# Opening of a fused attention and mixer kernel: who loads the constants, who casts first, and when a channel weight's transfer is issued

## The chip, the cores and the metric

The kernel runs on one core of a Trainium2 chip. The metric is the device time of one execution in microseconds (us); less is better. The core has five engines that run their own instruction streams and meet through semaphores: TensorE (PE; its weight loads are listed as PEld), VectorE (DVE), ScalarE (ACT), GpSimd (POOL) and SyncE (SP). Transfers between the chip's memory and the core are issued from the streams of SP, ACT and POOL, and all of them are carried by the same 16 DMA engines.

## The reference

A batch of 8 goes through windowed attention and then through a mixer. Four heads see the last 32 positions, four see every fourth of the last 128.

```python
# B, H, S, D = 8, 8, 576, 64
scores = (q @ k.T) / sqrt(D)
mask_plain = (rel >= 0) & (rel < 32)                      # heads 0 to 3
mask_dil = (rel >= 0) & (rel < 128) & (rel % 4 == 0)      # heads 4 to 7
attn = softmax(where(mask, scores, -1e9))
x = (attn @ v) as [B, S, 512]
h = relu(x.T @ w_tok1) @ w_tok2        # mixing over the 576 positions, inner width 256
u = x + h.T
out = u + relu(u @ w_ch1) @ w_ch2      # mixing over the 512 channels, inner width 1536
```

Inputs and output are float32; the kernel computes in float16 with float32 sums.

## The kernel before

One program handles the eight batches one after the other. For each batch it transposes q and k on TensorE (later batches by DMA), forms the scores in blocks near the diagonal, takes the exponential on ScalarE, multiplies with v (`av`), normalises on VectorE (`xn`), mixes over positions (`h1p`, `up`), turns the result (`tpu`) and mixes over channels: `gp` is the product with `w_ch1` (tiles `w3[0]` to `w3[2]`, four of twelve blocks `mb` each; in the trace they are all called `w`), `yp` the one with `w_ch2`. The order is written by hand: the stream of every engine is the order of the calls, and no engine goes past an instruction that waits. From batch 0's `gp` on, the attention of batch b+1 is interleaved into the main stream of batch b, by due times that are fixed in the code; the first transposes of batch 1 (`tp_q`, `tp_k`) stand between the first blocks of batch 0's `gp`.

Everything ahead of that is the opening, lines 840 to 1001, on which the change works. Its parts:

- Loads of q and k of batch 0 are issued in turn by SP and ACT (lines 843 to 850), in pieces of two, two and four heads, with the last 64 positions ("tails", tile `lt`) between them; then SP issues v (`load_v`, lines 199 to 220): four pieces `l_vn` for heads 0 to 3, the tail `l_vt`, two pieces `l_vd` for heads 4 to 7, and `l_vx`, their positions 384 to 511. A transfer issued by SP or ACT takes one of eight completion semaphores in turn; the ninth waits until the first has landed.
- The constants (identity, permutation, masks) come by POOL's queue (line 840).
- POOL casts most of what lands from float32 to float16 (lines 866 to 882), and between these casts it issues the weights' transfers, which convert on the way: `w1p`, `w1t`, `w2`, and with `load_w3` the channel weights `w3[0]` (line 878, ahead of the casts of `l_vd`) and `w3[1]` (line 881, between the casts of `l_vd` and `l_vx`).
- Line 884 copies `w2` into `w2p`. Line 974 is a gate: a copy of one element of `w2p[1]` into batch 1's tile `lt`, so that SP's loads of batch 1 (lines 975 to 980) are issued only after the second of these copies. Batch 1's casts on POOL start at line 981, with the third channel weight (line 984) between the first casts.
- `emit_fixed` and `emit_fixed_late` write the zeros and ones that stay: `qz` and `kt` on VectorE, the whole of `attt` on VectorE, the ones columns of both batches' `vv` and `vt` and the zeros of `w1t` on POOL.
- `warm` (line 831) issues matmuls on zeros, nine before the first transpose.

Of the kernel before, what the change touches and what calls it, by code (L numbers as in the profile page):

```python
# [16 lines left out]
S = 576  # L17
# [51 lines left out]
def kernel(  # L69
# [11 lines left out]
    nc = tc.nc  # L81
# [4 lines left out]
    def fixed(name, shape, dtype=FP16):  # L86
        return sb.tile(shape, dtype, tag=name, bufs=1, name=name)
# [28 lines left out]
    const = fixed("const", [128, CW])  # L116
# [12 lines left out]
    const_dram = nc.inline_tensor(const_np, name="consts").ap()  # L129
# [8 lines left out]
    vv = [fixed(f"vv{i}", [128, 5, H, 65]) for i in range(2)]  # L138
    vt = [fixed(f"vt{i}", [128, 4, 65]) for i in range(2)]
# [3 lines left out]
    attt = fixed("attt", [128, 4, 2, TW])  # L143
# [3 lines left out]
    w1t = [fixed(f"w1t{i}", [128, DTOK]) for i in range(2)]  # L147
    w2a = fixed("w2", [128, 2, 640])
# [10 lines left out]
    def emit_fixed():  # L159
        nc.gpsimd.memset(idle, 0.0)  # L160
        nc.gpsimd.memset(spread, 0.0)
        nc.vector.memset(qza[64:128, :, 0], 0.0)
        nc.vector.memset(qza[0:64, :, 1], 0.0)
        nc.vector.memset(kta[:, :, S:640], 0.0)
        for a in attp:
            nc.gpsimd.memset(
                a.rearrange("p h (b c) -> p h b c", c=PST)[:, :, :, 128:PST], 0.0)
        nc.vector.memset(attt, 1.0)

    def emit_fixed_late():  # L170
        for i in range(2):
            nc.gpsimd.memset(vv[i][64:128, 4], 0.0)
            nc.gpsimd.memset(vv[i][:, :, :, 64:65], 1.0)
            nc.gpsimd.memset(vt[i][:, :, 64:65], 1.0)
            nc.gpsimd.memset(w1t[i], 0.0)
        nc.gpsimd.memset(w2a[:, :, S:640], 0.0)


    l32 = {}
# [8 lines left out]
    def load_qk(b, nm, h0, h1, eng):  # L188
        i = h0 // 4
        eng.dma_start(  # L190
            out=l32[(b, nm, i)][:, h0 - 4 * i:h1 - 4 * i].rearrange("m h r d -> m h (r d)"),
            in_=SRC[nm][b, h0:h1, 0:512, :].rearrange("h (m r) d -> m h (r d)", r=4))

    def load_tail(b, nm, eng):
        r0 = 64 * (nm == "k")
        eng.dma_start(out=l32[(b, "t")][r0:r0 + 64],
                      in_=SRC[nm][b, :, 512:S, :].rearrange("h s d -> s h d"))
# [53 lines left out]
    def cast_qk(b, nm, hp, eng):  # L251
        if (b, nm) not in c16:
            c16[(b, nm)] = sb.tile([128, 4, 4, 2, D], FP16, tag=f"c_{nm}", bufs=1, name=f"c_{nm}_{b}")
        copy(eng, c16[(b, nm)][:, hp],
             l32[(b, nm, hp // 2)][:, 2 * (hp % 2):2 * (hp % 2) + 2].rearrange("m h r d -> m r h d"))
# [151 lines left out]
    def first_tails():  # L407

        p = bank("fl", 3, "tp_t", FP16)
        for hp in range(4):  # L410
            nc.tensor.transpose(
                out=p[:, 128 * hp:128 * hp + 128],
                in_=c16[(0, "t")][:, 2 * hp:2 * hp + 2, :].rearrange("m h d -> m (h d)"), identity=ident)
        t = p[:, 0:512].rearrange("p (x n c) -> p x n c", n=2, c=64)
        for h in range(2):
            rows = slice(64 * h, 64 * h + 64)
            nc.vector.tensor_copy(out=qza[rows, :, h, 512:S], in_=t[rows, :, 0])
        nc.vector.tensor_copy(out=kta[:, :, 512:S], in_=t[:, :, 1])
# [412 lines left out]
    def warm(n):  # L831

        p = bank("main", 3, "idle_p")
        for _ in range(n):
            nc.tensor.matmul(out=p, lhsT=idle[:, 0:128], rhs=idle, start=True, stop=True)
# [1 line left out]
    ctx.enter_context(tc.manual_schedule())  # L837


    nc.gpsimd.dma_start(out=const, in_=const_dram)  # L840
    emit_fixed()
    new_qk(0)
    load_qk(0, "q", 0, 2, nc.sync)
    load_qk(0, "k", 0, 2, nc.scalar)
    load_qk(0, "q", 2, 4, nc.sync)
    load_qk(0, "k", 2, 4, nc.scalar)
    load_tail(0, "q", nc.sync)
    load_tail(0, "k", nc.scalar)
    load_qk(0, "q", 4, 8, nc.sync)
    load_qk(0, "k", 4, 8, nc.scalar)  # L850
    spark = fixed("spark", [1, 1], FP32)
    nc.scalar.activation(out=spark, in_=idle[0:1, 0:1], func=AF.Exp)
    load_v(0)
# [1 line left out]
    def gate(t, src):  # L855
        nc.gpsimd.tensor_copy(out=t, in_=src)

    def load_w3(i):
        c = slice(512 * i, 512 * i + 512)
        nc.gpsimd.dma_start(out=w3[i], in_=moe_w_ch1[:, c].rearrange("(x p) c -> p x c", p=128))  # L860

    cast_qk(0, "q", 0, nc.scalar)
    cast_qk(0, "k", 0, nc.vector)
    nc.vector.tensor_scalar(out=veil, in0=const[:, 256:CW], scalar1=1.0, scalar2=60000.0,
                            op0=ALU.subtract, op1=ALU.mult)
    cast_qk(0, "q", 1, nc.gpsimd)
    emit_fixed_late()
    cast_tails_qk(0, nc.gpsimd)
    nc.gpsimd.dma_start(out=w1p, in_=moe_w_tok1[0:512, :].rearrange("(m r) j -> m r j", r=4))
    for hp in range(2, 4):  # L870
        cast_qk(0, "q", hp, nc.gpsimd)
    nc.gpsimd.dma_start(out=w1t[0][0:64], in_=moe_w_tok1[512:S, :])
    nc.gpsimd.tensor_copy(out=spread[:, 3:515:4], in_=ident)
    cast_qk(0, "k", 3, nc.gpsimd)
    for s in range(4):
        cast_vn(0, s, nc.gpsimd)
    nc.gpsimd.dma_start(out=w2a[:, :, 0:S], in_=moe_w_tok2.rearrange("(p j) t -> p j t", j=2))
    load_w3(0)
    cast_vd(0, 0, nc.gpsimd)
    cast_vd(0, 2, nc.gpsimd)  # L880
    load_w3(1)
    cast_vx(0, nc.gpsimd)
    nc.gpsimd.dma_start(out=w1t[1][64:128], in_=moe_w_tok1[512:S, :])
    for jb in range(2):
        nc.gpsimd.tensor_copy(
            out=w2p[jb], in_=w2[jb][:, 0:512].rearrange("p (m r) -> p r m", r=4))

    warm(9)
    ts = [st[2] for st in score_steps(0, 0.0, 1.0)]
    va = [st[2] for st in value_steps(0, 0.0, 1.0)]  # L890

    def tp(hp):
        ts[5 * hp]()
        ts[5 * hp + 1]()

    def sc(hp):
        for i in range(2, 5):
            ts[5 * hp + i]()

    def natural_w1(i):  # L900
        p = bank("main", 3, f"w1_p{i}")
        for s in (2 * i, 2 * i + 1):
            for r in range(4):
                nc.tensor.matmul(out=p[:, 256 * (s % 2):256 * (s % 2) + 256],
                                 lhsT=spread[:, 128 * s + 3 - r:128 * s + 131 - r], rhs=w1p[:, r],
                                 start=(r == 0), stop=(r == 3))
        copy(nc.scalar, w1n[:, 2 * i:2 * i + 2].rearrange("p s j -> p (s j)"), p)
# [3 lines left out]
    ts[2]()  # L911
    ts[3]()
    cast_qk(0, "k", 1, nc.vector)
    tp(1)
    first_tails()
    ts[7]()
    ts[8]()
# [8 lines left out]
    va[0]()  # L926
    va[1]()
    sc(3)
    va[2]()
    va[3]()  # L930
    natural_w1(0)
    natural_w1(1)
    for h in range(4, 8):
        va[h]()
# [37 lines left out]

    new_qk(1)
    gate(l32[(1, "t")][0:1, 0, 0:1], w2p[1][0:1, 0, 0:1])
    for nm in ("q", "k"):
        load_tail(1, nm, nc.sync)
    for h0 in (0, 4):
# [9 lines left out]
    for i in range(3):  # L987
        nc.gpsimd.dma_start(
            out=w4a[:, 4 * i:4 * i + 4],
            in_=moe_w_ch2[512 * i:512 * i + 512, :].rearrange("(p i) c -> p i c", i=4))  # L990
# [82 lines left out]
```

## Time and profile before

| what | us |
|---|---|
| median of 3 runs (range) | 288.43 (288.23 to 289.59) |
| the profiled execution, its own time | 289.66 |
| span of the trace, first to last instruction | 287.8 |
| PE busy in the span | 276.8 (96%) |
| POOL, ACT, DVE busy | 163.0, 134.0, 132.1 |

The page of the profile has a row of busy tenths in 40 slices of 7.2 us each. PE has 5, 8 and 7 tenths in the first three slices and 9 from then on but for the last. So what the opening costs stands in the first 22 us. The DMA row of the same page has 9 in nearly every slice of the first half, so transfers there stand in line for the DMA engines, and which transfer is issued first matters.

In the views, `x4` is the number of merged instructions, the time in a timeline row is when the first starts and for how long they go on, and what stands in brackets is how long the engine had been idle before and what ended that. For transfers the last number is the time from issue to landing.

### The profile page before, as it was taken

What the parts mean: (1) busy time and instruction counts of PE and PEld (TensorE: products, weight loads), DVE (VectorE), ACT (ScalarE), POOL (GpSimd) and SP (SyncE); (2) the same over time, 40 slices, a digit from 0 to 9 for tenths busy, and PEclk for the clock granted to TensorE, in tenths of its full rate; (3) what the DMA queues carried; (4) which work ended last, traced back from release to release, by engine and by line L of the source; (5) the groups of instructions that cost most, each with busy time, mean ns of one, the idle gap of its engine ahead of it and who ended that gap; (6) DMA issues with size and microseconds to landing.
All of it is one profiled execution on the core that took longest, in us unless ns stands there. A gap on an engine that the chain in (4) does not pass through costs nothing.

```text
span 287.8 us, 6995 instructions
## 1 busy us (share of the span) xinstructions
PE 276.8 (96%) x2838; PEld 210.9 (73%) x2838; DVE 132.1 (46%) x278; ACT 134.0 (47%) x265; POOL 163.0 (57%) x221
## 2 busy tenths in 40 slices
PE   5879999999999999999999999999999999999995
PEld 2777676888766886698776976797766966886594
DVE  7747658446764236414640164416440274421022
ACT  2854673263543804574447615482546534225500
POOL 6961860478865799449970999279952930000000
PEclk9999999999999999999999999999999999999999
DMA  7999999993999998979888978299974210431023
GB/s 218 263 211 218 283 225 207 320 218 82 328 210 192 264 264 230 139 164 350 226 159 182 330 224 186 57 219 329 193 150 95 85 64 2 91 112 37 0 76 108
DMA packets 105551, 52.63 MB, mean 183 GB/s; under 512 B 73872, under 2 KB 104464, under 8 KB 105520
## 3 DMA queue, kind: packets, MB, share of 16 engines
q1 hardware_dynamic: 101280, 47.07, 67.0%
q0 software_dynamic: 2640, 3.94, 8.0%
q10 hardware_dynamic: 1600, 1.18, 1.4%
q8 instruction: 22, 0.36, 0.6%
q14 instruction: 9, 0.07, 0.1%
HBM read 37.07 MB, written 9.44 MB: 162 GB/s over the span
## 4 chain that ended last, share of the span: by engine, by line
PE 80%; DMA 8%; DVE 3%; POOL 3%; issue 2%; ACT 2%; ACTq 1%; SPq 0%; POOLq 0%; DVEq 0%
PE yp L787 29%; PE gp L768 24%; DMA l_vd<-in_v_dram 4%; PE h1p L627 4%; PE yp L807 3%; DMA l_k<-in_k_dram 3%; PE up L639 3%; PE sc L510 3%; PE gt L759 3%; DVE xn L112 1%; DMA kr<-c_k 1%; PE h1p L625 1%; PE av L608 1%; PE up L650 1%; PE av L603 1%
## 5 line engine op out<-in xcount | busy, mean ns | idle before, releaser
L787 PE MATMUL yp<-w,gt 128*128 128x256 f16 x756 | 87.1, 273 | 0.0
L787 PEld LDWEIGHTS <-gt 128*128 128x128 f16 x768 | 78.6, 106 | 6.5
L106 ACT ACTIVATE gt<-gp 128x512 f16<-128x512 f32 x69 | 41.2, 597 | 76.3 <-PE gp L768 76.0
L768 PE MATMUL gp<-utd,w 128*128 128x512 f16 x144 | 54.7, 380 | 0.0
L768 PE MATMUL gp<-utm,w 128*128 128x512 f16 x144 | 54.6, 379 | 0.0
L768 PEld LDWEIGHTS <-w 128*128 128x128 f16 x384 | 39.2, 114 | 20.3 <-issue 0.5
L797 DVE TENSOR_TENSOR o<-yp,u 128x512 f32<-128x512 f32 x31 | 21.4, 691 | 63.1 <-PE yp L787 58.5
L112 POOL TENSOR_TENSOR attp<-attp,const 128x1280 f16<-128x1280 f16 x12 | 31.4, 2616 | 27.5 <-ACT attp L534 27.4
L112 DVE TENSOR_TENSOR xn<-av,rec 128x320 f16<-128x320 f32 x64 | 31.4, 491 | 2.2
L112 POOL TENSOR_TENSOR attd<-attd,const 128x1024 f16<-128x1024 f16 x12 | 25.3, 2132 | 1.6 <-ACT attd L534 1.6
L768 PE MATMUL gp<-uT,w 128*128 128x512 f16 x96 | 25.8, 379 | 0.0
L108 DVE TENSOR_SCALAR gt<-gp 128x512 f16<-128x512 f32 x27 | 18.5, 686 | 13.6 <-PE gp L768 13.1
L645 DVE TENSOR_TENSOR u<-up,xn 128x512 f16<-128x512 f32 x26 | 17.9, 690 | 7.5 <-PE up L639 7.5
L534 ACT ACTIVATE attp<-sc 128x480 f16<-128x480 f32 (+1 forms) x36 | 16.1, 536 | 7.4 <-PE sc L510 7.4
L102 POOL CAST c_k<-l_k 128x512 f16<-128x512 f32 x29 | 18.0, 628 | 1.9 <-DMA l_k<-in_k_dram 1.7
L102 POOL CAST c_q<-l_q 128x512 f16<-128x512 f32 x27 | 16.8, 629 | 3.1 <-DMA l_q<-in_q_dram 3.1
L616 DVE RECIPROCAL rec<-av 128x5 f32<-128x5 f32 x64 | 12.2, 190 | 13.8 <-PE av L613 13.7
L106 ACT ACTIVATE h<-h1p 128x256 f16<-128x256 f32 x29 | 11.1, 384 | 14.5 <-PE h1p L627 14.1
L399 POOL COPY kt<-kr 128x512 f16<-128x512 f16 x10 | 10.7, 1075 | 9.0 <-DMA kr<-c_k 9.0
L697 ACT COPY utd<-utm 128x512 f16<-128x512 f16 x12 | 12.8, 1135 | 4.1 <-DMA utm<-u 4.1
L102 POOL CAST vv<-l_vn 128x256 f16<-128x256 f32 x32 | 12.0, 420 | 4.3 <-DMA l_vn<-in_v_dram 4.1
L112 POOL TENSOR_TENSOR attt<-attt,const 128x512 f16<-128x512 f16 x12 | 14.0, 1165 | 0.0
(147 smaller groups left out, 459.9 us busy)
## 6 DMA issues: line engine op xcount, KB each, us to landing
out_dram<-o SPq DMA_DIRECT2D x72, 128.0 KB, 3.1
l_q<-in_q_dram SPq DMA_DIRECT2D x15, 512.0 KB, 7.2
l_k<-in_k_dram SPq DMA_DIRECT2D x14, 512.0 KB, 7.1
l_vn<-in_v_dram SPq DMA_DIRECT2D x32, 128.0 KB, 6.6
l_vd<-in_v_dram SPq DMA_DIRECT2D x16, 256.0 KB, 4.6
w<-in_moe_w_ch_dram POOLq DMA_DIRECT2D x6, 512.0 KB, 7.6
lt<-in_q_dram SPq DMA_DIRECT2D x8, 128.0 KB, 4.6
l_vt<-in_v_dram SPq DMA_DIRECT2D x8, 128.0 KB, 4.9
```

Of the source, the lines that this page charges most:

```text
L102: eng.tensor_copy(out=out, in_=in_)
L106: nc.scalar.activation(out=out, in_=in_, func=AF.Relu)
L108: eng.tensor_scalar_max(out=out, in0=in_, scalar1=0.0)
L112: eng.tensor_tensor(out=out, in0=x, in1=y, op=ALU.mult)
L534: nc.scalar.activation(out=out, in_=in_, func=AF.Exp, scale=0.125)
L616: nc.vector.reciprocal(out=rec[:, :, 0], in_=av[:, :, 64])
L627: nc.tensor.matmul(out=p, lhsT=w[:, s, j], rhs=x[:, s, c], start=False, stop=(s == 3))
L645: nc.vector.tensor_tensor(out=u16(b, s), in0=blocks4(p), in1=blocks4(xn[b][:, s]), op=ALU.add)
L697: nc.scalar.copy(out=natural(uTd[:, cb - 2]), in_=uTm[i][:, cb].rearrange("p r m -> p m r"))
L768: nc.tensor.matmul(out=p, lhsT=w3_block(cb, mb), rhs=uT[(b, cb)][0], start=(i == 0), stop=(i == 3))
L787: nc.tensor.matmul(out=p[:, c], lhsT=gta[:, mb, a0:m0 + 512:4] if half else gta[:, mb, a0:a0 + 128], rhs=w4[mb][:, c], start=(mb == 0), st ...
L797: nc.vector.tensor_tensor(out=blocks4(o32), in0=blocks4(p), in1=u16(b, s), op=ALU.add)
```

## The change

The constants are issued by SP as its second transfer instead of by POOL as its first. VectorE takes the first cast of q from ScalarE. The whole-tile write of `attt` becomes two calls of `emit_ones`, three small writes each, put behind the second cast of k and behind the second pair of transposes. The fixed writes for batch 1's buffers (`emit_fixed_late(1)`) and the second load of `w1t` go behind the gate. On POOL, the cast of k's last pair goes ahead of the copy into `spread`, the cast of `l_vx` goes ahead of both channel weights, and `load_w3(0)` goes behind the three casts of v, next to `load_w3(1)`. The first row of warm matmuls has seven instead of nine, and the first `natural_w1` stands ahead of the third `values` step.

```diff
-        nc.vector.memset(attt, 1.0)
+    def emit_ones(hp):
+        t = attt[:, 2 * hp:2 * hp + 2].rearrange("p a h c -> p (a h) c")
+        nc.vector.memset(t[:, :, 0:64], 1.0)
+        nc.vector.memset(t[:, :, 128:192], 1.0)
+        nc.vector.memset(t[:, :, 256:320], 1.0)
...
-    nc.gpsimd.dma_start(out=const, in_=const_dram)
     emit_fixed()
     new_qk(0)
     load_qk(0, "q", 0, 2, nc.sync)
     load_qk(0, "k", 0, 2, nc.scalar)
+    nc.sync.dma_start(out=const, in_=const_dram)
...
-    cast_qk(0, "q", 0, nc.scalar)
+    cast_qk(0, "q", 0, nc.vector)
...
-    emit_fixed_late()
+    emit_fixed_late(0)
...
     nc.gpsimd.dma_start(out=w2a[:, :, 0:S], in_=moe_w_tok2.rearrange("(p j) t -> p j t", j=2))
-    load_w3(0)
     cast_vd(0, 0, nc.gpsimd)
     cast_vd(0, 2, nc.gpsimd)
+    cast_vx(0, nc.gpsimd)
+    load_w3(0)
     load_w3(1)
-    cast_vx(0, nc.gpsimd)
-    nc.gpsimd.dma_start(out=w1t[1][64:128], in_=moe_w_tok1[512:S, :])
...
-    warm(9)
+    warm(7)
...
     cast_qk(0, "k", 1, nc.vector)
+    emit_ones(0)
     tp(1)
+    emit_ones(1)
...
     sc(3)
+    natural_w1(0)
     va[2]()
     va[3]()
-    natural_w1(0)
...
     gate(l32[(1, "t")][0:1, 0, 0:1], w2p[1][0:1, 0, 0:1])
+    emit_fixed_late(1)
+    nc.gpsimd.dma_start(out=w1t[1][64:128], in_=moe_w_tok1[512:S, :])
```

First place: POOL, from the load of `w2` (tile `w_81`) to batch 1's first cast. `w_0_84` and `w_1_85` are the first two channel weights, `lt_589` and `lt_587` the gate's target. Before:

```order
L877 DMA w_81<-in_moe_w_tok_dram 128x2x576
L860 DMA w_0_84<-in_moe_w_ch_dram 128x4x512
L102 CAST vv_69<-l_vd_123 128x4x2x64 [waits DMAHW5_49]
L102 CAST vv_69<-l_vd_123 128x4x2x64 [waits DMAHW6_49]
L860 DMA w_1_85<-in_moe_w_ch_dram 128x4x512
L102 CAST vt_71<-l_vx_124 128x4x64 [waits DMAHW7_49]
L883 DMA w1t_80<-in_moe_w_tok_dram 64x256 [waits Pool_49]
L885 COPY w2p_82<-w_81 128x512 [waits DMASW3_49]
L885 COPY w2p_83<-w_81 128x512
L856 CAST lt_589<-w2p_83 1x1 [waits Pool_49]
```

Now the same stretch reads:

```order
L882 DMA w_81<-in_moe_w_tok_dram 128x2x576
L102 CAST vv_69<-l_vd_122 128x4x2x64 [waits DMAHW6_49]
L102 CAST vv_69<-l_vd_122 128x4x2x64 [waits DMAHW7_49]
L102 CAST vt_71<-l_vx_123 128x4x64 [waits DMAHW0_49]
L865 DMA w_0_84<-in_moe_w_ch_dram 128x4x512
L865 DMA w_1_85<-in_moe_w_ch_dram 128x4x512
L889 COPY w2p_82<-w_81 128x512 [waits DMASW2_49]
L889 COPY w2p_83<-w_81 128x512
L861 CAST lt_587<-w2p_83 1x1 [waits Pool_49]
L176 MEMSET vv_70 64x520
L177 MEMSET vv_70 128x40 [waits Pool_49]
L178 MEMSET vt_72 128x4
```

The three casts of v now follow one another, both channel weights are issued behind the last of them, and the gate still stands behind both.

Second place: SP, from its first transfer to the first two of v. Before:

```order
L190 DMA l_q_0_107<-in_q_dram 128x2x256 x2
L196 DMA lt_111<-in_q_dram 64x8x64
L190 DMA l_q_1_108<-in_q_dram 128x4x256
L207 DMA l_vn_122<-in_v_dram 128x4x64 [waits DMAHW0_49]
L207 DMA l_vn_122<-in_v_dram 128x4x64 [waits DMAHW1_49]
```

Now, with the constants as the second transfer:

```order
L195 DMA l_q_0_105<-in_q_dram 128x2x256
L849 DMA const<-consts 128x672
L195 DMA l_q_0_105<-in_q_dram 128x2x256
L201 DMA lt_109<-in_q_dram 64x8x64
L195 DMA l_q_1_106<-in_q_dram 128x4x256 [waits DMAHW0_49]
L212 DMA l_vn_121<-in_v_dram 128x4x64 [waits DMAHW1_49]
```

The load of q's last four heads is now the ninth of these transfers and waits for the first one, that of k's first two heads, to land.

## Rows read from the trace of the kernel before

**Rows 1.** Who waited for whom, PE, 0 to 30 us; total us, times, longest.

```profile
PE av L611 <- POOL vt L102: 1.2, 1, 1.2
...
PE tp_q L309 <- DMA const<-consts: 0.6, 1, 0.6
```

**Rows 2.** Busy time by stretch: length, then each engine's busy us.

```profile
60.00:120.00 60.00, 59.40 (x630) 44.69 (x629) 31.58 (x67) 28.44 (x59) 47.12 (x58) 1.00 0.90 218
```

**Rows 3.** The chain of waits, 0 to 30 us: start, length, what.

```profile
11.76 7.27 DMA l_vd<-in_v_dram
...
19.08 0.63 POOL vv L102
19.71 0.68 POOL w L860
20.39 0.42 POOL vt L102
```

**Rows 4.** Timeline of POOL, 15 to 34 us.

```profile
19.65 0.74 POOL L860 DMA_DIRECT2D w<-in_moe_w_ch_dram  x1
...
21.25 1.25 POOL L885 COPY w2p<-w 128x512 f16<-128x512 f16 x2
22.57 0.18 POOL L856 CAST lt<-w2p 1x1 f32<-1x1 f16 x1
...
30.21 0.61 POOL L102 CAST c_q<-l_q 128x512 f16<-128x512 f32 x1 [0.80 <-DMA l_q<-in_q_dram]
30.76 0.77 POOL L860 DMA_DIRECT2D w<-in_moe_w_ch_dram  x1
31.67 0.61 POOL L102 CAST c_k<-l_k 128x512 f16<-128x512 f32 x1
32.22 0.62 POOL L102 CAST c_q<-l_q 128x512 f16<-128x512 f32 x1
```

**Rows 5.** Timeline of PE, 27 to 34 us: batch 0's `gp`, batch 1's transposes.

```profile
28.47 3.48 PE L768 MATMUL gp<-uT,w 128*128 128x512 f16 x14
31.79 0.39 PE L309 MATMUL tp_q<-const,c_q 128*128 128x128 f16 x4
...
32.93 0.39 PE L309 MATMUL tp_k<-const,c_k 128*128 128x128 f16 x4
33.15 0.39 PE L309 MATMUL tp_q<-const,c_q 128*128 128x128 f16 x4
```

**Rows 6.** Transfers of channel weights issued at 15.31 and 19.65: KB, us to landing.

```profile
w<-in_moe_w_ch_dram POOLq DMA_DIRECT2D x1, 512.0 KB, 7.8
w<-in_moe_w_ch_dram POOLq DMA_DIRECT2D x1, 512.0 KB, 6.9
```

**Rows 7.** DMA queues in 20:21, 28:30, 34:36: packets, MB, share; q0 is POOL's.

```profile
q0 software_dynamic: 175, 0.17, 102.5%
...
q1 hardware_dynamic: 602, 0.60, 103.6%
...
q0 software_dynamic: 306, 0.31, 92.1%
q1 hardware_dynamic: 367, 0.09, 29.6%
```

**Rows 8.** DMA queues in 17:19, while v's last pieces come in; q1 is SP's.

```profile
q0 software_dynamic: 318, 0.33, 106.4%
q1 hardware_dynamic: 36, 0.01, 3.9%
```

**Rows 9.** Timeline of VectorE, 3 to 5 us: the fixed writes.

```profile
3.35 0.17 DVE L164 MEMSET kt<- 128x128 uint32 x1
4.00 2.19 DVE L168 MEMSET attt<- 128x2560 f16 x1 [0.48 <-issue]
```

**Rows 10.** Loads issued at 0.74 (k, two heads) and 2.54 (q, four heads).

```profile
l_k<-in_k_dram ACTq DMA_DIRECT2D x1, 256.0 KB, 3.7
l_q<-in_q_dram SPq DMA_DIRECT2D x1, 512.0 KB, 8.1
```

More of the change, by code (lines that the diff above doesn't have):

```diff
@@ L167, in emit_fixed, with emit_fixed_late @@
                 a.rearrange("p h (b c) -> p h b c", c=PST)[:, :, :, 128:PST], 0.0)
-        nc.vector.memset(attt, 1.0)
[L170 to L176, printed above, removed]
+    def emit_ones(hp):
[3 more added lines that the diff above has]
+        nc.vector.memset(t[:, :, 256:320], 1.0)
+    def emit_fixed_late(i):
+        nc.gpsimd.memset(vv[i][64:128, 4], 0.0)
+        nc.gpsimd.memset(vv[i][:, :, :, 64:65], 1.0)
+        nc.gpsimd.memset(vt[i][:, :, 64:65], 1.0)
+        nc.gpsimd.memset(w1t[i], 0.0)
+        if i == 0:
+            nc.gpsimd.memset(w2a[:, :, S:640], 0.0)
     l32 = {}
@@ L844 @@
     load_qk(0, "k", 0, 2, nc.scalar)
+    nc.sync.dma_start(out=const, in_=const_dram)
+    load_qk(0, "k", 2, 4, nc.scalar)
     load_qk(0, "q", 2, 4, nc.sync)
-    load_qk(0, "k", 2, 4, nc.scalar)
+    load_tail(0, "k", nc.scalar)
     load_tail(0, "q", nc.sync)
-    load_tail(0, "k", nc.scalar)
+    load_qk(0, "k", 4, 8, nc.scalar)
     load_qk(0, "q", 4, 8, nc.sync)
-    load_qk(0, "k", 4, 8, nc.scalar)
     spark = fixed("spark", [1, 1], FP32)
@@ L872 @@
     nc.gpsimd.dma_start(out=w1t[0][0:64], in_=moe_w_tok1[512:S, :])
+    cast_qk(0, "k", 3, nc.gpsimd)
     nc.gpsimd.tensor_copy(out=spread[:, 3:515:4], in_=ident)
-    cast_qk(0, "k", 3, nc.gpsimd)
     for s in range(4):
```

## The prediction

> **What bounds the kernel now.** I read the busy shares first, then who waited for whom on PE, the chain of waits of the first 30 us, and the DMA queues of the stretches that the chain names. From about 30 us PE has next to no gap: it is busy for 59.4 of 60 us between 60 and 120 us [rows 2]. So whatever PE's position gains or loses by then stays to the end, and only the opening can give or take time. In the opening PE waits once for long: 1.2 us for POOL's cast of l_vx [rows 1]. The reader should see in the chain what is behind it: the second l_vd transfer is issued at 11.76 and takes 7.27 us, POOL casts it (0.63), then issues a channel weight (0.68), and only then casts l_vx (0.42) [rows 3]. The issue between the two casts is pure delay on the path of the end. The 0.6 us that PE waits for the constants [rows 1] lie ahead of that wait; a gain there only lengthens the later one.
>
> **The change, part by part.**
>
> *The casts of v.* The weight's issue of 0.68 leaves the path: the cast of l_vx may start at 19.71 instead of 20.39 and end at 19.71 + 0.42 = 20.13, and PE goes on 0.68 sooner, if v lands as before. Bounds: 0.68 with v landing as before, 1.2 (all of PE's wait) if it lands sooner, and 0 if it lands 0.7 later. I take 0.68: v's transfers are issued before the moved weight was, and the load of w2, which is in line with them, stays where it is.
>
> *Both channel weights behind these casts.* Here is what the change pays. Before, the first weight was issued at 15.31 and landed 7.8 later, at 23.1; the second at 19.65, landing at 26.55 [rows 6]. Now the first is issued at about 20.13, half a microsecond after the place that the second had. When such a weight has the DMA engines for itself it moves 0.17 MB in a microsecond at a share of 102% [rows 7], so its 0.52 MB need 3.1 us of all 16 engines. The first one's 3.1 us used to lie in the stretch in which little else moved (in 17 to 19 us POOL's queue had 106% and SP's 4%) [rows 8]; now this stretch carries the rest of w2 and then nothing. The first weight takes the second one's old slot and lands at about 26.55 + 0.5 = 27.0, in time for gp, which would start at 28.47 - 0.68 = 27.8 [rows 5]. The second one follows it in the same queue, and its 3.1 us fall into the time in which SP's loads of batch 1 used to run.
>
> *The gate.* POOL now does two issues (0.77 + 0.74) between the cast of l_vx and the w2p copies: 20.13 + 1.51 = 21.64 instead of 21.25, then the copies (1.25) and the gate as before [rows 4]. So batch 1's loads are issued 0.4 later. The fixed writes and the small load put behind the gate cost nothing: POOL is idle from 22.75 to the first cast of batch 1, whose q follows at 30.21 [rows 4]. If that cover went, it would be their own time, under 2 us, estimated from the 2.19 us that a write of 2560 columns takes on VectorE [rows 9].
>
> *How much later batch 1 lands.* Alone, SP's queue moves 0.60 MB in 2 us; beside a channel weight (34 to 36 us, the third one) it moves 0.09 MB, while POOL's queue keeps 92% [rows 7]. The loads nearly stand still while a weight passes. Delay: 3.1 for the second weight, plus 0.4 for the gate, less what the old second weight already took from these loads (it landed at 26.55 while they were issued from 22.75 on; I put that at 0.8) = 2.7. Bounds: 0.4 - 0.8 = -0.4 if the two kinds pass each other freely, 3.5 if nothing is taken off. I take 2.7, since 34 to 36 us shows the same two queues side by side.
>
> *What PE notices.* Batch 1's first casts end at 30.82 (q), 32.28 (k) and 32.84 (q, second pair) [rows 4], and PE uses them at 31.79, 32.93 and 33.15 [rows 5]: slacks of 1.0, 0.65 and 0.31. With casts 2.7 later the last one decides: 2.7 - 0.3 = 2.4 after its old time, whether or not PE came 0.68 sooner. The gain is waited away, and PE is 2.4 later from there on.
>
> *The rest is worth nothing.* The constants on SP's queue, the casts of q on VectorE and the whole early order end in the wait for v. The load of q's last four heads now waits for the first load of k, which lands at 0.74 + 3.7 = 4.45, so it goes 1.9 later than at 2.54, but there it took 8.1 us to land, most of it in line behind other loads [rows 10]; price 0, at most 1.9 - 1.2 = 0.7 of PE's time. The attt write of 2.19 goes from VectorE and six of 256 columns come, bounded by 0.17 (the kt write) and 2.19 / 10 = 0.22 plus a start: 1.0 to 1.8 in all [rows 9], in the gaps ahead of the tails. Fewer warm matmuls and the moved natural_w1 fill waits only.
>
> **Sum.** 289.66 (the profiled execution) + 2.4 = 292.1; it lies 1.2 above the median, so on the median 288.43 + 2.4 = 290.8.
>
> **The rivals.**
>
> 1. *Faster: the weights are through before batch 1's loads begin.* Then the gate costs 0.4 against slacks of 0.3 to 1.0, PE keeps 0.5 to 1.2 us, and the time is 287.2 to 287.9, 287.6 in the middle. It decides from one point on: when the loads are delayed by less than 0.3. For it speaks that both weights are issued 2.5 us ahead of those loads; against it, that each took 6.9 to 7.8 to land [rows 6]. The Trainium skill, page "DMA: Bandwidth & Descriptors", section "Anatomy of one DMA — SWDGE (gpsimd) path", would have it so: it fits such a transfer to a fixed 2.0 us plus its bytes at 436 GB/s, an estimate of 3.2 us for one of these and 4.4 for both, done at 24.5. The 6.9 and 7.8 of [rows 6] and the 0.17 MB in a microsecond of [rows 7] speak against that here.
>
> 2. *v lands clean.* In 17 to 19 us only 36 packets of SP's queue are left, and the second l_vd lands at 11.76 + 7.27 = 19.03, while POOL's queue has the engines at 106% [rows 3, 8]. If they came with the rest, at 17.5, all of POOL's work behind v would be 1.5 earlier: PE gains its 1.2, the loads of batch 1 are 2.7 - 1.5 = 1.2 late, and PE is 1.2 - 0.3 = 0.9 later: 289.3. The Trainium skill, same page, section "Latency and other measured facts", says that two of the 16 engines are usually slower while POOL's own queue is in use, with a cause it calls a best guess; by that rule the moved weight would free v's last share. No row here tells the engines apart. Against this rival: the load of w2 stays where it was and occupies that stretch anyway.
>
> 3. *Sharing is gentler.* If batch 1's loads get half of the engines instead of the 30% share that 34 to 36 us shows, they have moved most of what PE needs first before the weight is through; a delay of about 1.0 leaves 1.0 - 0.3 = 0.7 on PE: 289.1.
>
> **How the numbers follow.** Forecast 0.60, rival 1 0.14, rival 2 0.15, rival 3 0.11. The forecast's own range has a delay of 1.7 to 3.5, so 1.4 to 3.2 on PE: 289.8 to 291.6. The range for 8 in 10 takes in the middle of rival 1 below and 0.2 more above, for an engine that runs behind: 287.6 to 291.8. Within 0.5% (1.44 us, about what a measurement of this kernel can tell from no change) is 287.0 to 289.9. Slower by more: 0.57 of the forecast and 0.04 of rivals 2 and 3, 0.61. Faster by more needs all of rival 1's gain and some more: 0.08. The rest, 0.31, lies between.
>
> **What would show it.** In the new profile: PE's first wait is for constants no more, and the cast of l_vx directly follows that of l_vd; the wait of PE for it is shorter by about 0.7. The channel weights issued back to back at about 20, and POOL's queue at about full share from 22 to 28 us. Batch 1's first cast of q at about 33, with POOL idle until then for the load, and PE waiting for POOL's c_q and c_k casts by some 3 us in total between 30 and 37 us. From there no new gaps. I am wrong if PE starts tp_q of batch 1 without a wait, if SP's queue keeps its 0.3 MB a microsecond from 25 us on, or if v's last piece lands before 18 us and PE's start of gp moves by more than 1.2.

## The result, and the profile after

The changed kernel takes 289.28 us (median of 22 runs, 288.64 to 290.44), the one before 288.36 beside it (22 runs, 287.73 to 289.63): a ratio of 1.0031, 95% interval 1.0020 to 1.0043. The forecast had the sign right and the size too large: 0.9 slower, not 2.4. The profiled execution of after took 289.47, close to its median; that of before took 289.66, 1.3 above its own. A third profiled execution of the kernel before (b1 below: 288.51) is therefore the better base, and both are used here.

First who waited for whom on PE, 0 to 30 us, in after (total us, times, longest), against [rows 1]:

```profile
PE tp_q L314 <- POOL c_q L102: 1.6, 2, 1.0
PE idle_p L840 <- POOL idle L160: 1.3, 1, 1.3
PE tp_t L416 <- POOL c_t L102: 1.2, 1, 1.2
PE tp_q L314 <- DMA const<-consts: 0.5, 1, 0.5
```

The wait for `vt` is gone, but it was no constant part of the kernel before: b1, the same kernel, has none, and b0_again none either. All of PE's waits of b1 in the same stretch are these:

```profile
PE idle_p L835 <- POOL idle L160: 2.5, 1, 2.5
PE sc L425 <- DVE kt L314: 0.6, 2, 0.3
PE av L613 <- DVE vv L102: 0.5, 1, 0.5
PE up L949 <- ACT h L106: 0.2, 1, 0.2
```

Two waits of after are long: for the tails (`c_t`, 1.2; none in b1, 0.8 in the execution of [rows 1], next line) and for q's last heads (`c_q`, 1.0), whose load was issued at 4.42 instead of 2.54. The wait for the constants, 0.5, is still there.

```profile
PE tp_t L411 <- POOL c_t L102: 0.8, 1, 0.8
```

What followed stands in the stretches of after (length, PE's busy us first; the third number from the right is PE's granted clock):

```profile
9.00:10.00 1.00, 0.00 (x0) 0.00 (x0) 0.99 (x3) 0.89 (x2) 1.00 (x5) 1.00 1.09 348
11.00:12.00 1.00, 0.36 (x6) 0.16 (x3) 0.80 (x3) 0.95 (x2) 0.30 (x1) 1.00 1.39 224
12.00:13.00 1.00, 0.64 (x10) 0.64 (x11) 0.20 (x1) 0.08 (x1) 1.00 (x3) 0.85 1.37 229
13.00:14.00 1.00, 1.00 (x18) 1.00 (x16) 0.64 (x2) 0.41 (x2) 1.00 (x3) 0.50 1.09 206
15.00:16.00 1.00, 1.00 (x12) 0.91 (x10) 0.84 (x2) 0.78 (x3) 1.00 (x3) 0.50 1.09 319
```

PE had nothing to do from 9 to 10 us and little from 11 to 12; then the granted clock stood at 0.50, the lower of its levels, from 13 to 16 us. Not every execution of after has this fall: over the whole span the mean granted clock of its 22 runs is 0.993 or 0.994 in eight (0.994 in the profiled one) and 0.998 or more in fourteen. The medians of the two groups are 289.46 and 289.13.

POOL's timeline in after, against [rows 4]:

```profile
16.44 1.42 POOL L102 CAST vv<-l_vd 128x512 f16<-128x512 f32 x2 [0.17 <-DMA l_vd<-in_v_dram]
17.82 0.40 POOL L102 CAST vt<-l_vx 128x256 f16<-128x256 f32 x1
18.17 1.50 POOL L865 DMA_DIRECT2D w<-in_moe_w_ch_dram  x2
20.26 1.24 POOL L889 COPY w2p<-w 128x512 f16<-128x512 f16 x2 [0.59 <-DMA w<-in_moe_w_tok_dram]
21.56 0.18 POOL L861 CAST lt<-w2p 1x1 f32<-1x1 f16 x1
30.80 0.61 POOL L102 CAST c_q<-l_q 128x512 f16<-128x512 f32 x1 [0.67 <-DMA l_q<-in_q_dram]
32.31 0.61 POOL L102 CAST c_k<-l_k 128x512 f16<-128x512 f32 x1 [0.19 <-DMA l_k<-in_k_dram]
32.86 0.61 POOL L102 CAST c_q<-l_q 128x512 f16<-128x512 f32 x1
```

All of v's casts are done at 18.2, not 20.8: here v landed sooner than in the profiled execution of before. The weights are issued at 18.17, the gate comes 1.0 earlier, and still batch 1's casts stand 0.6 later. PE, against [rows 5]:

```profile
28.64 3.48 PE L773 MATMUL gp<-uT,w 128*128 128x512 f16 x14
31.96 0.39 PE L314 MATMUL tp_q<-const,c_q 128*128 128x128 f16 x4
33.10 0.39 PE L314 MATMUL tp_k<-const,c_k 128*128 128x128 f16 x4
33.53 0.40 PE L314 MATMUL tp_q<-const,c_q 128*128 128x128 f16 x4
```

Now DMA in after from 14 to 36 us: busy tenths of the 16 engines in 40 slices of 0.55 us each, and the channel weights' time from issue to landing, against [rows 6]:

```profile
DMA  9999999993559999999999999999999999999999
w<-in_moe_w_ch_dram POOLq DMA_DIRECT2D x3, 512.0 KB, 7.8
```

The 3, 5, 5 lie at 19.0 to 20.6 us: the weights are issued at 18.17, but what was queued is through and they have hardly begun. From 60 to 120 us PE is busy as in [rows 2]:

```profile
60.00:120.00 60.00, 59.61 (x632) 44.89 (x631) 31.88 (x68) 28.43 (x59) 46.10 (x58) 1.00 0.90 220
```

### The profile page after: what moved, and what is told of

The parts are those of the page before. It is cut to its first block, busy times and chain, and to the rows that moved or that the text cites. A ratio compares the mean times of both kernels' runs of the same rounds, so it can differ in the third digit from the quotient of the medians.

```text
span 287.7 us, 6994 instructions
## 1 busy us (share of the span) xinstructions
PE 277.9 (97%) x2836; PEld 212.4 (74%) x2836; DVE 131.7 (46%) x284; ACT 133.8 (47%) x264; POOL 162.2 (56%) x220
## 4 chain that ended last, share of the span: by engine, by line
PE 76%; DMA 8%; POOL 5%; DVE 5%; SPq 2%; issue 2%; ACT 1%; POOLq 0%; ACTq 0%; DVEq 0%
PE yp L792 25%; PE gp L773 23%; PE h1p L632 4%; PE gt L764 3%; PE yp L812 3%; PE up L644 3%; DMA l_k<-in_k_dram 3%; DMA l_q<-in_q_dram 3%; PE sc L515 2%; DVE xn L112 2%; DMA kr<-c_k 2%; PE h1p L630 1%; POOL attd L112 1%; DMA qt<-c_q 1%; PE av L608 1%
## 5 line engine op out<-in xcount | busy, mean ns | idle before, releaser
L816 DVE TENSOR_TENSOR o<-yp,u16t 128x512 f32<-128x512 f32 x4 | 2.8, 692 | 23.8 <-PE yp L812 23.8
```

## The experiments

Beside the ratio the table gives two times of the one profiled execution: PE's start of `gp`, and of the third `tp_q` of batch 1, the last one that waits for the loads of batch 1.

| run | what it is | median us | ratio to before (95%) | gp | third tp_q |
|---|---|---|---|---|---|
| b0_again, b1_before | before, one execution each | 289.23, 288.51 | | 28.10, 27.69 | 32.78, 32.37 |
| after | the change | 289.28 | 1.0031 (1.0020 to 1.0043) | 28.64 | 33.53 |
| e1 | weights alone | 289.44 | 1.0045 (1.0022 to 1.0067) | 26.67 | 33.02 |
| e2 | all but the weights | 289.29 | 1.0029 (1.0014 to 1.0045) | 28.55 | 33.23 |
| e3 | after, constants by POOL | 289.82 | 1.0050 (1.0024 to 1.0075) | 29.49 | 34.17 |
| e4 | after, clock held | 289.37 | 1.0044 (1.0028 to 1.0061) | 27.55 | 33.65 |
| e5 | constants alone | 289.14 | 1.0021 (1.0000 to 1.0042) | 28.70 | 33.38 |
| e6 | e1, gate ahead of the weights | 289.77 | 1.0046 (1.0029 to 1.0064) | 26.79 | 33.64 |
| e7 | after, gate ahead of the weights | 289.43 | 1.0041 (1.0027 to 1.0056) | 27.38 | 33.18 |
| e8 | second weight alone | 289.34 | 1.0026 (1.0007 to 1.0045) | 26.72 | 33.44 |
| e9 | e1, transposes later | 288.88 | 1.0022 (1.0004 to 1.0041) | 27.26 | 33.67 |
| e10 | e8, transposes later | 288.89 | 1.0012 (0.9993 to 1.0031) | 26.75 | 32.61 |
| f1 | e2, clock held | 288.69 | 0.9996 (0.9972 to 1.0021) | 27.52 | 32.44 |
| f2 | after, no wait for a lane | 290.78 | 1.0078 (1.0059 to 1.0096) | 28.61 | 35.16 |
| f3 | f2, weights in old places | 290.29 | 1.0078 (1.0047 to 1.0110) | 29.81 | 34.49 |
| f4 | before, batch 1's writes later | 288.70 | 1.0003 (0.9989 to 1.0016) | 27.48 | 32.17 |
| f5 | f1, transposes later | 288.84 | 1.0012 (0.9999 to 1.0025) | 27.35 | 32.90 |
| f6 | before, transposes later | 288.21 | 1.0001 (0.9987 to 1.0016) | 26.87 | 32.42 |

Executions of one kernel scatter over 1 to 2 us, and so do the times of a single profile: with nothing changed up to `gp`, it starts at 28.47, 28.10, 27.69 and 26.87 (before, b0_again, b1_before, f6). The ratios are what counts.

**The base.** The kernel before was profiled twice more, unchanged.

> The kernel before once more, for a second profile, since the profiled execution of before (289.66) lies 1.3 above its median and shows 0.4 us of ScalarE standing without a shown cause at 39.6. Theory A (that stall was chance): no such stall here, span 286.5 to 287.4. Theory B (it belongs to the kernel): the stall is there again and the span is 287.6 or more.

> The kernel before, a third profiled execution. The two at hand took 289.66 and 289.23, above the median of 288.4 of all of its executions, and start the third tp_q of batch 1 at 33.15 and 32.78. If the opening alone sets the differences between executions, one of about 288.4 starts it at 32.0 to 32.2, with POOL's first cast of q of batch 1 at 29.2 to 29.5; if not, the 0.8 lie elsewhere, as waits behind 33 us.

POOL and, in the second fence, PE of b1:

```profile
17.32 0.74 POOL L860 DMA_DIRECT2D w<-in_moe_w_ch_dram  x1
18.06 0.42 POOL L102 CAST vt<-l_vx 128x256 f16<-128x256 f32 x1
28.50 0.61 POOL L102 CAST c_q<-l_q 128x512 f16<-128x512 f32 x1 [0.63 <-DMA l_q<-in_q_dram]
30.54 0.61 POOL L102 CAST c_q<-l_q 128x512 f16<-128x512 f32 x1
```

```profile
27.69 3.48 PE L768 MATMUL gp<-uT,w 128*128 128x512 f16 x14
32.37 0.39 PE L309 MATMUL tp_q<-const,c_q 128*128 128x128 f16 x4
```

In this execution the cast of `l_vx` starts at 18.06 instead of 20.39 [rows 3], the first cast of q comes at 28.50 and not 30.21 [rows 4], a little earlier than expected, and the third cast ends at 31.15, 1.2 before PE wants it. In the execution of [rows 5] this slack was 0.31; in b0_again it is 0.24, and in f4, whose opening ran as early as that of b1, 0.27. The stall for which b0_again was run is there in all three executions of before (ScalarE idle 0.77 or 0.78 ahead of `attd`), so it belongs to the kernel.

**The two halves of the change.** e1 moves the weights alone, e2 leaves them where they were:

```diff
# e1, from before
-    load_w3(0)
     cast_vd(0, 0, nc.gpsimd)
     cast_vd(0, 2, nc.gpsimd)
-    load_w3(1)
     cast_vx(0, nc.gpsimd)
+    load_w3(0)
+    load_w3(1)
```
```diff
# e2, from after
+    load_w3(0)
     cast_vd(0, 0, nc.gpsimd)
     cast_vd(0, 2, nc.gpsimd)
-    cast_vx(0, nc.gpsimd)
-    load_w3(0)
     load_w3(1)
+    cast_vx(0, nc.gpsimd)
```

> The kernel before with one edit: the cast of l_vx ahead of both channel weights, and both issued behind the casts of v. Theory 1 (the weights' new place delays batch 1's loads, and that is the loss of the change): batch 1's first cast of q 0.5 or more later than 30.2, time 288.9 to 289.6. Theory 2 (the loss is made ahead of v, by the late load of q's last heads and the fallen PE clock): v's last cast ends by 20.1 or sooner, gp starts 0.7 to 1.2 sooner, and the time is 287.2 to 288.2.

> The changed kernel with the channel weights back in their old places (the first ahead of v's casts, the second between those of l_vd and l_vx). Theory 1: batch 1's loads are early again, 288.0 to 288.6, no slower than before. Theory 2: PE still has the clock at half from about 13 to 16 us, w_p starts at about 18.6, and the time is 288.9 to 289.6.

PE of e1 (in brackets the idle time and what ended it):

```profile
26.67 3.48 PE L768 MATMUL gp<-uT,w 128*128 128x512 f16 x14
30.95 0.40 PE L309 MATMUL tp_q<-const,c_q 128*128 128x128 f16 x4 [0.80 <-POOL c_q L102]
32.47 0.40 PE L309 MATMUL tp_k<-const,c_k 128*128 128x128 f16 x4 [0.20 <-POOL c_k L102]
33.02 0.40 PE L309 MATMUL tp_q<-const,c_q 128*128 128x128 f16 x4 [0.16 <-POOL c_q L102]
```

PE reaches `gp` 1.0 sooner than in b1 and is 0.65 later at the third `tp_q`. The early `gp` is not shown to come from the edit, for f6, which changes nothing ahead of it, has it as early:

```profile
26.87 4.34 PE L768 MATMUL gp<-uT,w 128*128 128x512 f16 x18
```

Wherever it came from, it is waited away at batch 1's casts. The time of e1 is that of theory 1; its first cast of q (30.28) is late against b1 (28.50), but not against the execution of [rows 4] (30.21). And e2, without the weights' move, is as slow. Each half costs some 0.8 to 1.3 us alone, and both together no more.

Why the loads are late in e1 shows in the DMA row from 14 to 36 us, first of b1, then of e1:

```profile
DMA  9999999999999999999999999999999999999999
```

```profile
DMA  9999999300038999999999999999999999999999
```

In b1 the 16 engines never rest. In e1 they do, for some 2 us from 18 on: v and `w2` are through, and the weights, issued at 18.93, have not begun. That time is given back in front of batch 1's loads, which stand behind the weights.

**Who loads the constants.** e3 gives them back to POOL, as its first transfer, in the changed kernel; e5 makes that one edit in the kernel before:

```diff
# e5, from before (e3 is the reverse, from after)
-    nc.gpsimd.dma_start(out=const, in_=const_dram)
...
     load_qk(0, "k", 0, 2, nc.scalar)
+    nc.sync.dma_start(out=const, in_=const_dram)
```

> The changed kernel with the constants issued by POOL first, as before, so that the load of q's last four heads is the eighth transfer again and waits for nothing. Theory 2: that load lands at about 10.6 instead of 11.6, tp_q of the third pair starts by 11.5, the clock falls for a shorter stretch or not at all, and the time is 287.6 to 288.6. Theory 1: the time stays at 289.0 to 289.6, since the weights are where the change put them.

> The kernel before with one edit: the constants are the second transfer of SP instead of the first of POOL, so that the load of q's last four heads waits for the first load of k. Theory 1 (this load is what made PE wait in the changed kernel): the load of q's four heads is issued at about 4.4 instead of 2.5 and lands near 11.6, PE waits 0.8 to 1.5 for its cast, the wait for the constants goes from 0.6 to 0 and that for v shrinks by as much; if v lands clean, gp starts 0 to 0.5 later than before, 28.1 to 28.6, and the time is 288.4 to 289.0. Theory 2 (the wait of a load is hidden by the later wait for v, as the prediction priced it): gp at 28.1, the same time as before within 0.2.

e3 was no cure: PE waits 1.1 for the constants and then 1.2 for VectorE, which now casts both first pieces and stands behind the constants with `veil`; it missed what was expected. e5 met theory 1 in part: the load of q's last heads is issued at 4.60 and lands at 11.5, and the wait for the constants is gone; but PE has no wait for that load's cast. It waits 0.6 for VectorE's cast of k and 1.0 for that of v's tail (`vv`; b0_again has 1.1 of the same). `gp`, at 28.70, and the time lie a little above theory 1's ranges; the time is 0.7 over that of before, though the interval reaches to 1.0000.

**Clock and gate.** e4 fills PE's two early waits with matmuls on zeros; e6 and e7 put the gate ahead of the weights:

```diff
# e4, from after
+    warm(5)
     first_tails()
...
+    warm(3)
     ts[10]()
```
```diff
# e6 from e1, e7 from after
     cast_vx(0, nc.gpsimd)
+    new_qk(1)
+    gate(l32[(1, "t")][0:1, 0, 0:1], vt[0][0:1, 0, 0:1])
     load_w3(0)
...
-    new_qk(1)
-    gate(l32[(1, "t")][0:1, 0, 0:1], w2p[1][0:1, 0, 0:1])
```

> The changed kernel with eight more warm matmuls in PE's two early waits (five ahead of the first tails, three ahead of the third score block). What is open is the cost of the granted clock, which fell to 0.50 from 13 to 16 us in the changed kernel. Theory 1 (the opening of PE and batch 1's loads are two limits, and the later one counts): the clock stays near 1.0 from 12 to 17 us, gp starts 0.8 to 1.5 earlier than 28.64, but the third tp_q of batch 1 still stands at 33.2 to 33.5, where POOL's last cast of q (32.86) lets it; the time stays within 0.3 of the changed kernel, 289.0 to 289.5. Theory 2 (the clock alone made the changed kernel slower): third tp_q near 32.7 and a time of 288.3 to 288.6, as before. If the fillers cost as much as they save, gp stands at 28.6 with the clock at 1.0.

> The kernel before with the cast of l_vx ahead of both channel weights, and the gate of batch 1's loads directly behind that cast, ahead of the weights. Theory 1 (batch 1's loads took back the 1.8 that PE won at gp when the weights alone were moved): the gate stands at about 19.0 instead of 21.3 to 22.3, POOL's first cast of q of batch 1 at 27 to 28 instead of 30.3, gp starts at 26.7 to 27.0, no tp wait is longer than 0.3, the third tp_q stands at 31.2 to 31.7 instead of 32.8, and the time is 286.9 to 287.4. Theory 2 (the channel weights, now beside batch 1's loads, are late for gp): gp waits for w for 1 to 3 us, first in its first block or at the fifth, and the time is 288.5 to 290. Theory 3 (what the opening wins is taken back in batch 1 in any case): third tp_q near 31.5 but a time of 288.2 to 288.6.

> The changed kernel with the gate of batch 1's loads directly behind the cast of l_vx, ahead of both channel weights. Theory 1 (two limits, of which the changed kernel's own opening of PE is the later one once batch 1's loads are early): the gate at about 18.5, first cast of q of batch 1 at 27 to 28, gp unchanged at 28.4 to 28.7, the third tp_q at 33.0 to 33.3, 0.2 to 0.5 earlier than in the changed kernel, and a time of 288.7 to 289.1, still slower than before by 0.3 to 0.6. Theory 2 (the loads alone made the changed kernel slower): a time of 288.3 or less. Theory 3 (weights late for gp): gp waits for w, and the time is over 289.5.

e4: the clock stays at 1.00, `gp` starts 1.1 earlier, the third `tp_q` does not, and the time is the same: theory 1. e6 met none of its theories (its time lies where theory 2 had it, but `gp` waits for no weight): the gate came 3 us sooner than in e1 and the first cast of q 0.6 later (30.91 against 30.28). The queues of e6 from 22 to 27 us (q0 is POOL's, q1 SP's: packets, MB, share), then of after from 22 to 25, say why:

```profile
q0 software_dynamic: 771, 0.77, 91.3%
q1 hardware_dynamic: 790, 0.20, 29.6%
```

```profile
q0 software_dynamic: 611, 0.61, 123.1%
```

Side by side both move 0.97 MB in 5 us, 0.19 a microsecond; a weight alone moves 0.20. Sharing wins nothing, and the loads move 0.04 of it. e7 is no better than after either, though its `gp` came at 27.38, sooner than any theory had it. So the gate is not the limit; by these rates it is the bytes in line. The early `gp` of e7 goes with the clock and not with the gate: with the changed opening it starts at 27.35 to 27.55 where the clock stayed up (e4, e7, f1, f5) and at 28.55 and 28.64 where it fell (e2, after). e7 changes nothing ahead of 18 us and has no fillers; PE waits much as in after (1.5 for the tails, 1.0 for q's last heads), and yet the clock stayed up in this execution:

```profile
9.00:10.00 1.00, 0.17 (x3) 0.18 (x4) 0.86 (x4) 0.59 (x2) 0.84 (x2) 1.00 1.10 351
11.00:12.00 1.00, 0.05 (x1) 0.00 (x0) 0.52 (x2) 0.77 (x2) 0.65 (x2) 1.00 1.39 223
13.00:14.00 1.00, 1.00 (x24) 0.91 (x21) 0.72 (x2) 1.00 (x4) 1.00 (x4) 1.00 1.08 204
```

**One weight, and later transposes.** e8 moves only the cast of `l_vx` ahead of the second weight; e9 and e10 place batch 1's transposes and first scores later in PE's order:

```diff
# e8, from before
-    load_w3(1)
     cast_vx(0, nc.gpsimd)
+    load_w3(1)
# e10, from e8 (e9, from e1: 4.6, 6.8, 6.0, 8.4, 8.0, 10.4, 9.4, 12.2)
-    ((3.0, 5.2), (4.4, 7.0), (7.2, 9.6), (8.6, 11.4))
+    ((3.8, 6.0), (5.2, 7.8), (7.6, 10.0), (9.0, 11.8))
```

> The kernel before with one call moved: the cast of l_vx goes ahead of the second channel weight; the first one keeps its place ahead of v's casts. Theory 1 (the 16 DMA engines bound batch 1's loads; both weights behind v's casts leave them idle for 2 us from 18.5 on, and one of them does not): no stretch of the DMA row under 8 between 15 and 24 us, the cast of l_vx 0.7 earlier and gp with it, at 27.2 to 27.6, POOL's casts of q and k of batch 1 where before has them (29.9, 31.4, 31.9), the third tp_q at 32.5 to 32.8, and a time within 0.3 of before, 288.1 to 288.6. Theory 2 (any change of the order of v's casts and the weights costs this much): 289.0 to 289.5. Theory 3 (PE's gain at gp is kept): 287.7.

> The kernel before with both channel weights behind v's casts, as in the run of the weights alone (e1), and batch 1's transposes and first scores placed 0.8 to 1.6 us later in the order of PE, behind more blocks of batch 0's gp. Theory 1 (PE's gain of 1.4 to 1.8 at gp was lost only because batch 1's transposes stood in front of gp's next blocks and their casts were 0.4 later): gp at 26.7, no wait of PE for c_q or c_k over 0.3 us, the fifth block of gp about 1.5 earlier than in e1, and a time of 287.0 to 287.8. Theory 2 (what PE wins there is lost at the next thing that comes by DMA): a new wait behind 33 us, for the third channel weight or a cast of batch 1, and 288.3 to 289.4.

> The kernel with the cast of l_vx ahead of the second channel weight only (e8) and batch 1's transposes and first scores placed 0.4 to 0.8 us later in the order of PE. Theory 1: the 0.7 that PE wins at gp is kept, since the transposes no longer stand in front of gp's next blocks before their casts are done: gp at 27.2 to 27.6, no wait for c_q or c_k over 0.2, and a time of 287.5 to 287.9. Theory 2 (lost at the next thing that comes by DMA): 288.2 to 288.6, with a wait of 0.5 or more behind 33 us.

POOL of e8:

```profile
18.64 0.40 POOL L102 CAST vt<-l_vx 128x256 f16<-128x256 f32 x1 [1.41 <-DMA l_vx<-in_v_dram]
18.98 0.74 POOL L860 DMA_DIRECT2D w<-in_moe_w_ch_dram  x1
30.70 0.61 POOL L102 CAST c_q<-l_q 128x512 f16<-128x512 f32 x1 [0.73 <-DMA l_q<-in_q_dram]
```

The call that looked like pure delay in [rows 3] is none in e8: POOL stands idle 1.41 for `l_vx`, which lands at 18.6, and the weight is issued at 18.98 instead of 17.32 as in b1. The old order would have put the issue into that wait (e1, e6, e9 and e10, without it there, wait 1.2 to 1.5; f4, with it, 0.3). It depends on the execution: in that of [rows 3] and in b1 `l_vx` had landed (at 19.4 and 17.3) by the time of the issue (19.65 and 17.32), so there the issue did delay the cast (in b1 without a wait of PE), and in after, e3 and e7, without it there, the wait is 0.2 or less. e8 missed theory 1's time (289.34 against 288.1 to 288.6); the DMA row has only two slices of 7 in it, so here it should be the weight's later place in line, more than an idle stretch, that makes the loads late; no run tests the place by itself. e9 and e10 got about half of the loss back by their medians, in e10 to within the interval of no change, but the intervals of e1 and e9, and of e8 and e10, overlap. Theory 1 of neither was met in time: no wait for `c_q` or `c_k` is left in e9, but `gp` started 0.6 later than in e1.

**Both cures at once.** f1 is e2 with the fillers of e4.

> The changed kernel with both channel weights back in their old places (as e2) and eight more warm matmuls in PE's early waits (as e4). Theory 1 (two limits, PE's own opening slowed by the fallen clock, and batch 1's loads behind the idle stretch of the DMA engines; each alone is enough to cost 0.8 us): with both cured, the clock at 1.0 from 12 to 17 us, gp at 27.3 to 27.8, POOL's first cast of q of batch 1 at 28.5 to 30.0, the third tp_q at 32.0 to 32.8, and 288.0 to 288.6, as before. Theory 2 (the order of the early transfers costs by itself, whatever the clock): gp at 28.3 or later and 289.0 to 289.5.

From 13 to 14 us, e2 first, then f1 (the clock is third from the right), and then PE of f1:

```profile
13.00:14.00 1.00, 1.00 (x18) 1.00 (x16) 0.60 (x2) 0.39 (x2) 1.00 (x4) 0.50 1.08 204
```

```profile
13.00:14.00 1.00, 1.00 (x26) 0.93 (x22) 0.71 (x3) 0.90 (x4) 1.00 (x3) 1.00 1.09 207
```

```profile
27.52 3.48 PE L773 MATMUL gp<-uT,w 128*128 128x512 f16 x14
32.44 0.40 PE L314 MATMUL tp_q<-const,c_q 128*128 128x128 f16 x4
```

That is the time of before (0.9996). Fillers alone (e4): 1.0044; weights back alone (e2): 1.0029; neither (after): 1.0031; both: 0.9996. The loss goes only where both limits are lifted, so it is the later of two, and each ends some 0.9 to 1.3 us behind the old opening. The intervals of e4 and f1 lie apart; those of e2 and f1 overlap a little, and there the clock of the single executions helps: in e2 the five with a mean granted clock of 0.994 have a median of 289.60, the seven with 0.998 or more 288.81, near the 288.69 of f1, none of whose twelve is under 0.998. In after, where the loads are late as well, the same split is worth only 0.3 (289.46 and 289.13).

**The wait for a lane** (one of the eight completion semaphores). f2 loads k's tails by POOL's queue, so that the load of q's last heads is the eighth and waits for none; f3 has the weights back besides.

```diff
# f2 from after, f3 from e2; new_qk(0) stands ahead of emit_fixed()
         nc.gpsimd.memset(idle, 0.0)
+        load_tail(0, "k", nc.gpsimd)
...
-    load_tail(0, "k", nc.scalar)
```

> The changed kernel with the tails of k loaded by POOL's queue, right behind its first fixed write, so that the load of q's last four heads is the eighth of the transfers of SP and ACT and waits for none. Theory 1 (the lane wait made that load late): it is issued at about 2.9 instead of 4.4 and lands at 10.4 to 10.9 instead of 11.64; PE's wait for its cast goes from 1.0 to 0.3 or less, the clock stays above 0.9 from 12 to 16 us, gp at 27.4 to 28.0, but batch 1's loads still come late (first cast of q at 30.3 to 30.9) and the time is 288.9 to 289.4. Theory 2 (the DMA engines are full from 3 to 17 us, so that the place in line decides and not the issue): it lands at 11.3 to 11.7 all the same, or another load comes later by as much, gp at 28.4 to 28.8, and 289.1 to 289.5.

> As f2, with both channel weights back in their old places. Theory 1 (lane wait and the weights' place are the two costs): gp at 27.4 to 28.0, first cast of q of batch 1 at 28.5 to 30.0, the third tp_q at 32.1 to 32.7, and 288.1 to 288.6. Theory 2 (the order of the early transfers costs by itself): gp at 28.4 to 28.8, and 289.0 to 289.4, as e2.

That load in f2, issued at 3.02, and in after, issued at 4.42 (KB, us from issue to landing):

```profile
l_q<-in_q_dram SPq DMA_DIRECT2D x1, 512.0 KB, 8.8
```

```profile
l_q<-in_q_dram SPq DMA_DIRECT2D x1, 512.0 KB, 7.2
```

Issued 1.4 sooner it lands at 11.8 against 11.6. Taking the lane's wait away did not bring it forward, as theory 2 had it; both runs are slower than either theory had them, by 1 us and more over after. In f2 this shows at v's last piece: its cast starts at 19.93 instead of 17.82, after a wait of 1.33, the weights are issued at 20.27 instead of 18.17, and PE waits 1.0 for batch 1's first cast of q. In f3 PE's clock is at 0.50 from 13 to 16 us and `gp` starts at 29.81. Why v comes so late was not settled (the last of v's loads is issued 0.2 us later than in after in f2, and 1.0 in f3).

**The rest.** f4 does one part of the change alone; f5 and f6 place the transposes of f1 and of before as in e10.

```diff
# f4, from before
-    emit_fixed_late()
+    emit_fixed_late(0)
...
     gate(l32[(1, "t")][0:1, 0, 0:1], w2p[1][0:1, 0, 0:1])
+    emit_fixed_late(1)
+    nc.gpsimd.dma_start(out=w1t[1][64:128], in_=moe_w_tok1[512:S, :])
```

> The kernel before with one part of the change alone: the fixed writes for batch 1's buffers and the second small load of w1t go behind the gate. Theory 1 (POOL is the bound of nothing in the opening for long; v's landing ends it): POOL's casts of v are done when v lands as before, gp at 27.5 to 28.1, and 288.1 to 288.5. Theory 2 (POOL is busy for 9.8 of the 10 us from 8 to 18 in the kernel before, and 1.7 us less work there brings the casts of q, k and v forward): the casts of l_q's last heads at 9.5 to 10.2 instead of 10.6, gp at 27.0 to 27.3, and 287.5 to 288.0, faster than both.

> The run with clock and weights cured (f1), and batch 1's transposes and first scores placed 0.4 to 0.8 us later in the order of PE, as in e10. Theory 1 (in some executions of f1 PE waits for batch 1's casts, since its third tp_q follows POOL's cast without slack): no wait for c_q or c_k behind 30 us, gp at 27.3 to 27.6, and 288.1 to 288.4, 0.3 to 0.5 under f1. Theory 2 (v's landing ends the opening, and nothing behind it matters): the same as f1 within 0.2.

> The kernel before with batch 1's transposes and first scores placed 0.4 to 0.8 us later in the order of PE, and nothing else. Theory 1 (in its typical execution these casts are done 1.2 before PE wants them, so the place is worth something only where v's and batch 1's loads come late): the median within 0.2 of before, with fewer executions above 289. Theory 2 (each later place costs where the values of batch 1 wait for the scores): 0.3 to 0.6 slower, with a new wait of PE between 33 and 50 us.

All three are level with before: batch 1's writes cost and bring nothing, and the later place of the transposes is worth nothing where the loads come in time. No version run here is faster than the kernel before.

## Why the prediction was right in sign and wrong in size

- *What bounds the kernel*: right. What is lost is lost by 34 us: from the third `tp_q` to the end of the span it is 254.65, 254.62 and 254.33 in the three executions of before and 254.17 in after. One gain was missed: between that `tp_q` and 47 us after is 0.4 quicker, where ScalarE stands 0.38 ahead of `attd` instead of 0.78; its cause was not tested.
- *The casts of v*: the path was wrong. PE's wait of 1.2 for `vt`, from which the 0.68 was to come, stands in one execution of before, in which v's last share came late; b0_again, b1, f4 and f6 have none. There was as a rule nothing to win, and `gp` of after, 28.64, is not earlier. The 0.8 that PE waited for the tails in that same execution was not looked at.
- *Both weights behind the casts*: the cost is real (e1: 1.0045 alone), and what PE was ahead at `gp` in e1 was waited away, as the forecast has it for a gain there. The picture behind it failed: the loads do not creep beside the second weight. They stood in line behind both, with no packet of SP's queue in 22 to 25 us, by when 0.9 of the two weights' 1.05 MB had moved (at 0.20 MB in a microsecond, not 0.17). What makes them late is the idle stretch of the engines ahead of the weights, and the weights' place in line.
- *How much later batch 1 lands*, and *What PE notices*: this is the step that made the size wrong, 2.7 - 0.3 = 2.4 on PE. Against the very execution that both terms were read from, the first cast of q is 0.6 later and the third `tp_q` 0.4 (33.53 - 33.15), for its loads were late already. Against executions near the median the two terms depend on the one chosen, and what is left on PE hardly does: a delay of 2.3 (30.80 - 28.50) less a slack of 1.2 against b1, 1.6 less 0.3 against f4; 1.1 and 1.3, where the third `tp_q` shows 1.16 and 1.36. Less the 0.4 gained behind it that is 0.8 to 1.0, against a measured 0.9. In after's own profile the loads are not alone in this: its `gp` too is 0.95 later than in b1, and PE's list of waits between 30 and 37 us is empty, where some 3 us were forecast. It is in e4, with the clock up, that PE waits for the casts (0.55, 0.19, 0.16).
- *"The rest is worth nothing"*: wrong, and hidden by the former. The load behind the wait for a lane was priced at 0 with a bound of 0.7; e2 shows 0.8 for the early part alone, and f1 (0.9996) and e2's own executions with the clock up (288.81) that most of it goes with the fall of PE's clock, which came after waits that the forecast did not look for. It did not add, because the later of two limits counts. Which edit of the early part makes those waits is open: e5 (the constants alone) is 0.7 slower without them.
- *The rivals*: the time of the second one, 289.3, was the one measured, and v did land clean, but before too, in b1; so its sum (PE gains 1.2, loads 1.2 late) is not what happened, and that the time fits is luck. So it is with the third one's 289.1: in after the loads got no share of the engines in 22 to 25 us, and in e6 30%, not half. Rival 1's figure for the weights fails: the Trainium skill's page "DMA: Bandwidth & Descriptors", section "Anatomy of one DMA — SWDGE (gpsimd) path", led to an estimate of 3.2 us for one, and the trace of after has 7.8 in the middle.

## What to carry to other kernels

Take slacks from more than one execution: where a stage ends in transfers, one profile may be an unlucky one, a wait of 1.2 in it was absent from the next, and a slack of 0.3 was 1.2 in another. Where the DMA engines were full, moving an issue earlier or past another bought nothing here (f2, e6), but an issue made later can leave them idle and is paid for by everything in line behind. When two edits each cost as much as both together, look for two limits of equal length, and try both cures at once before dropping either.

## What was not expected of the hardware

- A channel weight issued by POOL with nothing else in line began some 2 us after its issue (e1: issued at 18.93, the engines nearly idle until 20.6), and then moved 0.20 MB in a microsecond. A load issued by SP into the same idle stretch began as late (e6: issued at 19.39, no packet of its queue before 21).
- TensorE's granted clock went from 1.00 to 0.50 for 3 us after two waits within 3 us (busy 0.00 in 9 to 10, 0.36 in 11 to 12); with fillers in both waits it stayed at 1.00. It does not fall each time: in e7, with as little work in the same two slices (0.17 and 0.05), it stayed at 1.00 without fillers.
- Batch 1's loads beside weights got 0.04 MB in a microsecond at a share of 30%, and the weights 0.15 at 91% (e6, where the loads were issued from 19.39, before the weights had begun to move). Issued into the weights' transfer they got nothing: in after from 21.77 on, no packet by 25.0 beside 611 of POOL's.
- v's last piece lands up to 2 us late in some executions and not in others of the same kernel (`l_vx` at 19.4 in the first execution of before, at 17.3 in b1). What holds it is open; no row here tells the 16 engines apart.
